# Two group sums in place of seven: the combine weights of the first 96 cells in a fused agent-attention and soft-MoE kernel

## The chip, the cores and the metric

The kernel runs on one core of one Trainium2 chip. The metric is the device time of one execution in microseconds; the figure for a kernel is the median of its runs. The core has a matrix engine (TensorE, PE in the profile), three engines for elementwise work (VectorE or DVE, ScalarE or ACT, GpSimd or POOL), and a sync engine (SP) from which all the transfers of this kernel are issued. Each engine works through its own queue of instructions in order, and waits on semaphores for the others.

## The reference

Two stages follow each other. First attention through 49 agents for each of 4 batches of 11,456 tokens of width 128, then a soft mixture of experts over all 45,824 tokens, with 8 experts of 4 slots each, so 32 slots:

```python
def sm(a, b):                      # softmax of scaled scores over the last axis
    s = scale * (a @ b.transpose(0, 2, 1))
    s = s - s.max(-1, keepdims=True)
    e = np.exp(s)
    return e / (e.sum(-1, keepdims=True) + 1e-09)
agent_v = sm(agents, k) @ v        # agents read the keys and values
x = (sm(q, agents) @ agent_v)      # queries read the agents
logits = x @ phi                   # 45824 x 32
d = softmax of logits over tokens  # dispatch weights
slot_input = d.T @ x
slot_out = relu(slot_input @ w1) @ w2        # expert by expert
c = np.exp(logits - logits.max(1, keepdims=True))
c /= c.sum(1, keepdims=True) + 1e-09         # combine weights of a token
out = c @ slot_out
```

The change concerns the last but one line: the sum of a token's 32 combine weights, and the division by it.

## The kernel before, in words

Tokens are handled in cells of 128; a batch has 90 cells, the four have 360. The tile `x_all` (128 partitions x 360 cells x 32 slots, fp32) holds the logits of all tokens, a token being one partition of one cell, and later, in place, their combine weights.

**The main stage.** Key groups of up to 20 cells (steps named k...) compute the agents' view of the values of a batch; query groups of up to 16 cells (steps q...) compute scores, softmax and logits. The steps that matter below: `ks` scores of keys, `km` and `kM` their maximum, `kr`/`kR` the running maximum, `ku`/`ke` subtract and exponential, `kE` the product with the values, `kA` its accumulation; `qs` scores of queries, `qt` their transposition, `qm` maximum, `qu`/`qe`/`qw` subtraction on POOL, exponential on ACT and sum on DVE (for every other group; the others do these in one ACT step, `qE`), `qr`/`qR` the reciprocal of the sum, `qg` the scaling on POOL, `qp`/`qc` transposition, `ql` the logits, `qM` their column maximum, `qn` their move into `x_all`. Per token, `cr` takes the maximum of the 32 logits, `cu` (POOL) subtracts it, `ce` (ACT) takes the exponential: from then on the cell holds combine weights that are not yet normalised. Per round of one or two query groups (13 rounds), `r1` to `r4` find the maximum over tokens, `ru` (POOL), `re` (ACT) and `rg` (PE) build the partial slot inputs, and `rc` stores them.

**The last steps before the output** are a chain: `nm`, `wt` (weights of the rounds), `l0`, `f0`/`f1`/`f2` (rescale of the earlier batches), `gl`, `gm` and `l1` to `l4` (the slot inputs, into `si`), `d0` to `d2` (the dispatch denominator), then per half of the experts and half of the hidden width `mh` (first product), `mr` (ReLU), `mt` (transposition), `mc` (copy), `mo` (second product), `ms`, `sb` and `sd`, which leaves the slot outputs in `sob`. `fl` are transpositions without use in TensorE's queue. `w1` and `w2` load the experts' weights once the last key group has released its buffers.

**The output stage** goes over 25 chunks of cells, `CHUNKS = [4, 12] + [16] * 21 + [4, 4]`, `C0` being the first cell of each. Of a chunk, `o_sum` (three DVE instructions: the sum over 32 slots, the addition of 1e-9, the reciprocal) and `o_mul` (POOL, multiplies in place) normalise the weights, `o_tr` (DVE) transposes them into one of four `ct` tiles, TensorE multiplies with `sob` into a PSUM tile `po`, DVE and ACT copy it to `ot`, and the sync queue writes it out. In the loop at the end (L994 to L1008) sums and multiplications run three chunks ahead and transpositions one.

The first chunks do part of this earlier, as steps of the written order: `os` (o_sum) and `om` (o_mul) for `NORM = 7` chunks (cells 0 to 95), `ot` (o_tr) for `EARLY = 4`. The sums lie in seven tiles `cd` of the pool that takes the place of the key buffers.

**What sets the order.** All steps up to the output loop are listed by hand in the string `ORDER`, in the form step.part@index. The order of issue on each engine is the order of its steps in this list; `_order` only asserts that every step comes behind those it depends on. Semaphores between the engines follow from the data. So to move a step in the string is to move it in its engine's queue. The costs written beside the steps are not used for the order.

Lines that the profile names: L252 scores of keys (`sk`), L351 `kE` (`ev`), L466 `qs` (`sq`), L472 `qt`, L477 `qm`, L494 `qE`, L504 `qr`, L535 `ql` (`lq`), L547 `qM` (`cm`), L552 `qn`, L560 `cr`, L563 `cu`, L568 `ce`, L635 `ru` (`dt`), L648 `rg` (`gp`), L652 `rc`, L726 `wt`, L734 `gl` (`g_all`), L757 `f0` (`fd`), L786 `l4` (`si`), L805 `mh` (`hp`), L811 the ReLU on DVE (`hs`), L818 `mt` (`htp`), L852 to L854 `o_sum` (`cd`), L859 `o_mul`, L865 `o_tr` (`ct`), L1002 `po`, L1006 and L1007 the copies to `ot`, L1008 the output.

Of the kernel before, what the change touches and what calls it, by code (L numbers as in the profile page):

```python
# [53 lines left out]
kM@3 kt kA qp.0@0 kr qx@3 qr@2 kt qR@2 qc.0@0 kR qg.0@2 kr qc.1@0 kb kR kn qg.1@2 ka@4 kb ku.0
qp.0@2 ka@3 kn ku.1 ke.0 kx@5 qp.1@2 qc.0@2 ku.0 kE.0@3 qc.1@2 ku.1 ke.1 qs.0@3 ke.1 ke.0
qs.1@3 kv@5 qt.0@3 kE.1 qt.1@3 qm@3 ks.0@5 kA qu@3 cx ks.1@5 km.0@5 qx@4 qe@3 kE.0@4 km.1@5
qw@3 kE.1 kM@5 qr@3 qR@3 kt kx@6 qg.0@3 kA kr kg.1 qg.1@3 kg.2 qp.0@3 kh.1 kh.2 kg.3 qs.0@4
kh.4 kh.3 kb kv@6 ql@0 qt.0@4 kn ql@1 ku.0 qc.0@3 qn.0@0 qs.1@4 ke.0 qM.0@1 qn.1@0 qM.0@0
kE.0@5 ku.1 qx@5 qM.1@0 ke.1 ks.0@6 qt.1@4 qm@4 kx@7 kE.1 km.0@6 qE.0 qM.1@1 ql@2 r1@0 kA r2@0
qn.0@1 ks.1@6 qM.1@2 qM.0@2 qn.1@2 kv@7 r3@0 qE.1 qp.1@3 qn.0@2 ru.0@0 km.1@6 qs.0@5 kM@6  # L60
qn.1@1 kt qt.0@5 ru.1 ks.0@7 kr kR cr@1 re.0@0 qr@4 qR@4 qx@6 re.1 cu@1 kb qs.1@5 km.0@7 kn
qc.1@3 rg.0@0 ku.0 qg.0@4 ka@6 rg.1 ce@1 ku.1 ql@3 ke.0 qg.1@4 qt.1@5 qp.0@4 ke.1 kx@8 qn.0@3
ks.1@7 qM.1@3 rc@0 qc.0@4 qm@5 qM.0@3 qu@5 r1@1 kE.0@6 km.1@7 qe@5 kM@7 cr@2 r2@1 kE.1 kv@8
r3@1 qn.1@3 ru.0@1 cr@3 qs.0@6 kA cr@0 cu@2 re.0@1 qs.1@6 qt.0@6 cu@0 qw@5 rg.0@1 ce@2 qx@7 kt
qt.1@6 ks.1@8 ru.1 ce@0 kr kR qr@5 qR@5 ka@7 qm@6 kb ks.0@8 cu@3 re.1 r4@1 kx@9 r4@0 kn qE.0
# [1003 lines left out]
```

## Time and profile before

| | |
|---|---|
| median of 3 runs | 320.97 us (319.19 to 323.69) |
| the profiled execution | 321.17 us |
| its span, first to last instruction | 318.9 us |
| busy: PE, DVE, ACT, POOL | 266.3, 248.1, 189.4, 132.5 us |
| HBM read, written | 79.91 MB, 23.59 MB |
| w1 issued first | 217.33 us from the span's start |
| first output issued | 258.21 us |

The span is the profile's own time axis; the profiled execution's time is 2.3 us longer than it. A timeline row gives start, length, engine, line, operation, tiles as out<-in with their shapes, and, in brackets, how long the engine sat idle before it and what ended that wait. A row with x2 or more merges instructions that followed each other. A row of a window gives the window, its length, then the busy time (and count) of PE, its weight loads, DVE, ACT and POOL, TensorE's granted clock, and the busy share and rate of the transfers. Releasers are inferred.

### The profile page before, as it was taken

The page shows a single profiled execution, that of the slowest core. Times are in us where ns is not written, and L with a number is a line of the kernel's source. Part 1 is how long each engine was busy: PE and PEld are TensorE (multiplying, and loading weights), DVE is VectorE, ACT ScalarE, POOL GpSimd, SP SyncE. Part 2 cuts the span into 40 slices and gives each one's busy share as a digit, 9 for nine tenths or more (in the row PEclk, how much of TensorE's full clock was granted, in tenths as well). Part 3 has the DMA queues.
Part 4 walks back from the last instruction along what each step waited for, and adds up shares of the span by engine and source line. Part 5 has one row for each costly group of instructions (what it writes and reads, how often), then busy time and mean ns, then how long its engine had stood idle before and what let it go on. Part 6 is the DMA issues. An engine that isn't in the chain of part 4 may idle for free.

```text
span 318.9 us, 11055 instructions
## 1 busy us (share of the span) xinstructions
PE 266.3 (84%) x4522; PEld 169.4 (53%) x4522; DVE 248.1 (78%) x598; ACT 189.4 (59%) x623; POOL 132.5 (42%) x166
## 2 busy tenths in 40 slices
PE   3799999997698998988999998998898876766850
...
GB/s 250 400 402 390 398 396 402 401 397 400 394 250 376 399 393 368 301 260 295 377 377 264 252 360 384 244 175 237 419 141 3 2 164 422 415 415 420 420 419 286
DMA packets 31298, 104.20 MB, mean 327 GB/s; under 512 B 3601, under 2 KB 7825, under 8 KB 27537
## 3 DMA queue, kind: packets, MB, share of 16 engines
...
HBM read 79.91 MB, written 23.59 MB: 325 GB/s over the span
## 4 chain that ended last, share of the span: by engine, by line
PE 45%; DVE 26%; DMA 10%; ACT 9%; issue 5%; POOL 2%; SPq 0%; DVEq 0%; POOLq 0%; ACTq 0%
PE sk L252 10%; PE ev L351 8%; PE sq L466 8%; DMA out<-ot 7%; PE tp L522 5%; ACT pt L494 4%; PE po L1002 3%; DVE pt L472 3%; PE lq L535 3%; DVE kmx L305 2%; ACT ot L1007 2%; DVE cd L852 2%; DVE ot L1006 2%; DMA w1s<-w 2%; DVE mx L477 2%
## 5 line engine op out<-in xcount | busy, mean ns | idle before, releaser
L494 ACT ACTIVATE pt<-pt,mx 128x49 f32<-128x49 f32 x192 | 61.6, 329 | 10.2 <-DVE mx L477 10.2
L513 POOL TENSOR_TENSOR pt<-pt,rt 128x392 f32<-128x392 f32 (+1 forms) x48 | 38.7, 809 | 46.1 <-DVE rt L508 25.2
L252 PE MATMUL sk<-ag,kt 128*64 128x49 f32 x1440 | 51.7, 230 | 6.6 <-DMA kt<-kT 4.3
L252 PEld LDWEIGHTS sk<-ag,kt 128*64 128x64 f32 x1440 | 48.8, 145 | 11.6 <-DVE ag L183 4.1
L466 PE MATMUL sq<-qt,ag 128*32 128x512 f32 (+1 forms) x384 | 49.6, 607 | 1.8 <-DVE et L339 1.1
L1002 PE MATMUL po<-ct,sob 32*128 32x512 f32 (+2 forms) x200 | 37.8, 838 | 15.6 <-DVE ct L865 11.3
L351 PE MATMUL ev<-vt,et 128*64 128x129 f32 x720 | 46.8, 277 | 1.7 <-issue 1.4
L1007 ACT COPY ot<-po 128x1536 f32<-128x1536 f32 (+2 forms) x25 | 32.8, 1311 | 23.3 <-DVE ot L1006 23.2
L351 PEld LDWEIGHTS ev<-vt,et 128*64 128x64 f32 x720 | 40.3, 138 | 9.6 <-issue 5.6
L472 DVE STREAM_TRANSPOSE pt<-sq 128x512 f32<-128x512 f32 (+1 forms) x48 | 31.9, 669 | 12.5 <-PE sq L466 12.0
L635 POOL TENSOR_TENSOR dt<-x_all,mbs 128x512 f32<-128x512 f32 (+1 forms) x24 | 29.2, 1227 | 28.8 <-DVE mbs L626 24.9
L859 POOL TENSOR_TENSOR x_all<-x_all,cd 128x512 f32<-128x512 f32 (+2 forms) x25 | 24.0, 961 | 38.0 <-DVE cd L854 37.3
L482 POOL TENSOR_TENSOR pt<-pt,mx 128x784 f32<-128x784 f32 (+1 forms) x12 | 16.2, 1353 | 55.4 <-DVE mx L477 53.1
L494 ACT ACTIVATION_READ_ACCUMULATOR pt<-pt,mx 128x1 f32 x192 | 37.0, 193 | 0.0
L529 ACT COPY pT<-tp 128x512 f32<-128x512 f32 (+1 forms) x48 | 25.7, 557 | 13.1 <-PE tp L522 11.0
L1002 PEld LDWEIGHTS po<-ct,sob 32*128 32x128 f32 x200 | 10.8, 247 | 42.5 <-ACT ot L1007 42.1
L522 PE MATMUL tp<-cs,pt 128*128 128x128 f32 x180 | 27.9, 286 | 5.9 <-issue 4.2
L305 DVE TENSOR_REDUCE kmx<-sk 128x49 f32<-128x490 f32 x32 | 20.7, 658 | 13.8 <-PE sk L252 13.6
L344 ACT ACTIVATE et<-et 128x490 f32<-128x490 f32 x36 | 21.6, 619 | 11.2 <-DVE et L339 11.1
L522 PEld LDWEIGHTS tp<-cs,pt 128*128 128x128 f32 x180 | 19.5, 142 | 15.1 <-issue 9.0
L339 DVE TENSOR_TENSOR et<-sk,kmb 128x490 f32<-128x490 f32 x36 | 22.5, 653 | 2.9 <-ACT kmb L329 2.8
L1006 DVE COPY ot<-po 128x512 f32<-128x512 f32 (+2 forms) x25 | 15.7, 629 | 11.4 <-DMA out<-ot 7.5
...
## 6 DMA issues: line engine op xcount, KB each, us to landing
...
```

What stands on the lines that cost most here:

```text
L252: t_.matmul(sp[r:r + 64, c - c0, :], xt[:, P * c + r:P * c + r + 64], ag[:, b, 0:A], start=True, stop=True)
L305: v_.tensor_reduce(out=o_, in_=sp.rearrange("p c a -> p a c"), axis=AX.X, op=ALU.max)
L351: t_.matmul(k["ev"][o_:o_ + 64, :], k["e"][:, c, :], k["v"][:, c, :], start=c < 2, stop=c >= n - 2)
L466: t_.matmul(q["s", h][32 * r_:32 * r_ + 32, :nt], ag[:, b, 32 * h:32 * h + 32], q["x"][:, r_, :], start=True, stop=True)
L472: v_.transpose(out=q["pt"][:, :n, 32 * h:32 * h + 32], in_=q["s", h][:, :nt].rearrange("p (t a) -> p t a", a=32))
L494: s_.activation(out=x, in_=x, func=AF.Exp, bias=q["mx"][:, c:c + 1], accum_out=q["dn"][:, c:c + 1])
L513: nc.gpsimd.tensor_tensor(out=x, in0=x, op=ALU.mult, in1=q["rt"][:, c0:c1].unsqueeze(2).to_broadcast([P, c1 - c0, A]))
L522: t_.transpose(q["tp", h][:, (c - c0) // 2, :], q["pt"][:, c:c + 2, :].rearrange("p c a -> p (c a)"), ident)
L529: s_.copy(out=q["pT"][:, c0 // 2:c1 // 2, :], in_=q["tp", h][:, :(c1 - c0) // 2, :])
L635: nc.gpsimd.tensor_tensor(out=q["dt"][:, :n], in0=q["lt"][:, :n, :], op=ALU.subtract, in1=mbs[:, ri, :].unsqueeze(1).to_broadcast([P, n, S]))
L1002: t_.matmul(po[:, r, :32 * n], z["sob"][32 * r:32 * r + 32, :], z["ct", j][32 * r:32 * r + 32, :32 * n], start=True, stop=True)
L1007: s_.copy(out=ov[:, 1:4], in_=po[:, 1:4, :32 * n])
```

## The change

The seven `os` steps become two, `os@0` for cells 0 to 47 and `os@1` for 48 to 95. Each is one reduction over 48 cells, one addition and one reciprocal, into halves of a new tile `cds` of 96 columns that exists from the kernel's start; so the sums no longer depend on `ms`, the step that sets up the tiles in the key buffers' place. They depend on the `ce` of the query groups that begin below cell 48 or 96. Both stand in the middle of the main stage: `os@0` between `qp.1@7` and `km.1@12`, `os@1` between `ks.0@13` and `kA`. The seven `om` steps follow one by one in the main stage: `om@0` and `om@1` around the `ru` of round 3 and `cu@6`, `om@2` behind `qg.1@11`, and `om@3` to `om@6` behind `qg.1@12` to `qg.1@15`. `om` of chunk 0 to 2 needs the first sum alone, the others need both.

Of the early transpositions, `ot@0` and `ot@1` now stand directly behind `l4` (the slot inputs) and ahead of `d1`, `ot@2` behind the first ReLU on DVE (`mr@32`), `ot@3` behind `mc@42`. Before, `os@3` and `om@3` stood some way ahead of `nm`, and the other six sums, the other six `om` and the four `ot` between `nm` and the second expert product. The order of all other steps is the same. The chunks from 7 on, in the output loop, are done as before, with a ring of seven `cd` tiles.

```diff
...
-fl r4@11 qn.1@21 rg.0@10 qn.0@21 fl cr@21 ru.1 re.0@11 fl fl fl nm os@1 wt fl rg.0@11 cu@21
-re.1 l0 fl f0 os@6 rc@11 f1 fl rg.1 om@1 ce@21 os@4 fl rc@10 fl gl om@6 ot@1 gm l1 d0 fl om@4
-fl l2 cr@18 fl l3 f2 l4 d1 cu@18 os@2 mh@35 d2 cu@20 ce@18 os@5 mh@31 mr@36 os@0 om@5 ce@20
-mh@39 mr@32 om@0 mt@41 ot@3 mt@37 mc@42 cu@22 mh@44 mc@38 ot@0 om@2 mr@40 mo ce@22 mr@45 ot@2
-mt@46 mt@50 mc@47 zz mo mc@51 mo ms mo sb ms sb fl fl sd
...
+qp.1@7 os@0 km.1@12 kn qg.1@10 qp.0@10 kM@12 qc.1@7 ku.0 kt kx@14 qs.0@11 ke.0 ku.1 kr ql@7 ke.1
...
+qs.1@11 r3@3 r4@3 ru.1 qp.1@9 om@0 qt.1@11 kb qm@11 qc.1@9 qp.1@8 ru.0@3 kn re.1 qs.0@12 ku.0 kv@13
+qc.1@8 ku.1 cu@6 om@1 re.0@3 ql@9 qt.0@12 ql@8 ke.0 qM.0@9 rg.0@3 cu@7 ce@6 qM.1@8 rg.1 qM.0@8 ke.1
...
+r4@4 kE.1 cr@9 qx@14 qr@11 qR@11 re.1 cu@9 qt.1@12 ks.0@13 os@1 kA qm@12 qg.0@11 ce@9 qp.1@10
+km.0@13 qE.0 qg.1@11 om@2 qp.0@11 qn.0@8 ks.1@13 cr@8 ru.0@4 qs.0@13 kx@16 km.1@13 cu@8 re.0@4 kM@13
...
+qn.0@21 fl cr@21 ru.1 re.0@11 fl fl fl nm wt fl rg.0@11 cu@21 re.1 l0 fl f0 rc@11 f1 fl rg.1 ce@21
+fl rc@10 fl gl gm l1 d0 fl fl l2 cr@18 fl l3 f2 l4 ot@0 ot@1 d1 cu@18 mh@35 d2 cu@20 ce@18 mh@31
+mr@36 ce@20 mh@39 mr@32 ot@2 mt@41 mt@37 mc@42 ot@3 cu@22 mh@44 mc@38 mr@40 mo ce@22 mr@45 mt@46
+mt@50 mc@47 zz mo mc@51 mo ms mo sb ms sb fl fl sd
...
+    cds = keep.tile([P, C0[NORM]], F32, name="cds")
...
+    def o_sums(h):
+
+        n = C0[NORM] // 2
+        x = cds[:, n * h:n * h + n]
+        v_.tensor_reduce(out=x, in_=x_all[:, n * h:n * h + n], axis=AX.X, op=ALU.add)
+        v_.tensor_scalar(out=x, in0=x, scalar1=EPS, scalar2=None, op0=ALU.add)
+        v_.reciprocal(out=x, in_=x)
+        for j in range(NORM):
+            z["cd", j] = cds[:, C0[j]:C0[j] + CHUNKS[j]]
+
     def o_sum(j):
...
-        z["cd", j] = wl(f"cd_{j}", [P, CHUNKS[j]], tag="cd", bufs=NORM)
+        z["cd", j] = wl(f"cd_{j}", [P, CHUNKS[j]], tag="cd", bufs=7)
...
+    def done(c):
+        return [k for k in ops if k[0] == "ce" and
+                groups[k[1]][0] * NCELL + GROUPS[groups[k[1]][1]][0] < c]
+
+    n = C0[NORM] // 2
+    ss = [op("os", (h,), "V", 2300, lambda h=h: o_sums(h), deps=done(n * h + n)) for h in range(2)]
     for j in range(NORM):
-        ends_ = [k for k in ops if k[0] == "ce" and groups[k[1]][0] * NCELL <= C0[j] + CHUNKS[j]]
-        f = op("os", (j,), "V", 800, lambda j=j: o_sum(j), deps=ends_ + [ms])
-        f = op("om", (j,), "G", 1000, lambda j=j: o_mul(j), deps=(f,))
+        f = op("om", (j,), "G", 1000, lambda j=j: o_mul(j), deps=ss[:1 + (C0[j] + CHUNKS[j] > n)])
         if j < EARLY:
-            op("ot", (j,), "V", 650, lambda j=j: o_tr(j), deps=(f,))
+            op("ot", (j,), "V", 650, lambda j=j: o_tr(j), deps=(f, ms))
```

The lines of the string show where the steps stand; the string was broken into lines anew, so a line of the new one holds other words than the old line in its place.

More of the change, by code (lines that the diff above doesn't have):

```diff
@@ L54 @@
[L54 to L65, printed above, removed]
@@ new lines @@
+kR ka@1 kb qs.0@1 kn ku.0 kv@0 ke.0 ku.1 qs.1@1 qt.0@1 ke.1 kE.0@1 kx@2 qt.1@1 qm@1 qs.0@0 qu@1
+kE.0@0 qt.0@0 kx@4 qs.1@0 qe@1 kA kE.1 qw@1 qt.1@0 ks.0@2 qr@1 qR@1 qm@0 qg.0@1 qx@2 ks.1@2 km.0@2
+qE.0 qg.1@1 kA qp.0@1 km.1@2 ks.0@4 kv@2 kM@2 qc.0@1 qp.1@1 km.0@4 qE.1 kt qs.0@2 kr kR kb kx@3
+qt.0@2 qc.1@1 qs.1@2 qr@0 qR@0 kn qg.0@0 ka@2 ku.0 ku.1 ks.1@4 ke.0 qg.1@0 qt.1@2 ke.1 kv@3 qm@2
+kE.0@2 km.1@4 qE.0 qp.1@0 kM@4 ks.0@3 kv@4 ks.1@3 km.0@3 qE.1 kE.1 km.1@3 kM@3 kt kA qp.0@0 kr qx@3
+qr@2 kt qR@2 qc.0@0 kR qg.0@2 kr qc.1@0 kb kR kn qg.1@2 ka@4 kb ku.0 qp.0@2 ka@3 kn ku.1 ke.0 kx@5
@@ new lines @@
+qp.1@2 qc.0@2 ku.0 kE.0@3 qc.1@2 ku.1 ke.1 qs.0@3 ke.1 ke.0 qs.1@3 kv@5 qt.0@3 kE.1 qt.1@3 qm@3
+ks.0@5 kA qu@3 cx ks.1@5 km.0@5 qx@4 qe@3 kE.0@4 km.1@5 qw@3 kE.1 kM@5 qr@3 qR@3 kt kx@6 qg.0@3 kA
+kr kg.1 qg.1@3 kg.2 qp.0@3 kh.1 kh.2 kg.3 qs.0@4 kh.4 kh.3 kb kv@6 ql@0 qt.0@4 kn ql@1 ku.0 qc.0@3
+qn.0@0 qs.1@4 ke.0 qM.0@1 qn.1@0 qM.0@0 kE.0@5 ku.1 qx@5 qM.1@0 ke.1 ks.0@6 qt.1@4 qm@4 kx@7 kE.1
+km.0@6 qE.0 qM.1@1 ql@2 r1@0 kA r2@0 qn.0@1 ks.1@6 qM.1@2 qM.0@2 qn.1@2 kv@7 r3@0 qE.1 qp.1@3 qn.0@2
+ru.0@0 km.1@6 qs.0@5 kM@6 qn.1@1 kt qt.0@5 ru.1 ks.0@7 kr kR cr@1 re.0@0 qr@4 qR@4 qx@6 re.1 cu@1 kb
@@ new lines @@
+qs.1@13 qE.1 qt.0@13 rg.0@4 qt.1@13 rg.1 kt qm@13 ks.0@14 kv@16 kr ce@8 qu@13 kR qr@12 qR@12 qc.0@11
+kb qs.0@14 km.0@14 kn rc@4 ka@13 qc.1@10 ku.0 qg.0@12 qp.1@11 qe@13 kt ku.1 ql@10 qg.1@12 om@3
+qc.1@11 qx@15 kr ke.1 qp.0@12 kR qn.0@10 ke.0 qM.0@10 ql@11 qM.1@10 qc.0@12 kb kE.0@13 qM.0@11 kn
+qM.1@11 ka@14 r1@5 qn.1@10 kx@15 cr@10 r2@5 kE.1 r3@5 qn.0@11 ru.0@5 ku.0 qs.1@14 kA ke.0 r4@5
+qn.1@11 cr@11 re.0@5 ru.1 qs.0@15 qt.0@14 qx@16 cu@11 rg.0@5 re.1 qw@13 qs.1@15 cu@10 ce@11 qr@13
+qR@13 rg.1 qt.1@14 kE.0@14 qg.0@13 rc@5 ce@10 qm@14 qx@20 qg.1@13 om@4 ks.1@15 kA qE.0 qt.0@15
@@ new lines @@
+qt.1@15 kg.2 kg.1 ks.0@15 qm@15 kv@15 kh.2 kh.1 qu@15 qE.1 qs.0@16 km.0@15 km.1@15 qs.1@16 kM@15
+qt.0@16 kt kx@19 qp.0@13 kr kh.4 qe@15 qr@14 qR@14 kb qt.1@16 qp.1@13 qg.0@14 kn qc.0@13 ku.0 kg.3
+kv@19 qp.1@12 qg.1@14 om@5 qc.1@13 qw@15 qp.0@14 ke.0 qp.1@14 kh.3 qr@15 qm@16 qc.1@12 qx@17 ks.0@16
+qc.0@14 qR@15 qc.1@14 ku.1 qg.0@15 ql@13 qE.0 km.0@16 ql@14 qg.1@15 om@6 qn.0@13 qp.0@15 qn.1@13
+qM.1@14 ks.1@16 qn.1@14 qM.0@13 qn.0@14 qE.1 qM.0@14 ql@12 kx@17 km.1@16 kE.0@15 qM.1@12 qM.0@12
+kM@16 qn.1@12 kt qn.0@12 qs.0@17 ke.1 kr cr@12 qp.1@15 qc.0@15 qr@16 qt.0@17 kE.1 qc.1@15 kR qR@16
@@ new lines @@
+kb qs.0@19 qt.1@18 qe@17 kn qm@18 qs.1@19 qx@21 qt.0@19 qE.0 rg.1 qw@17 ks.0@18 ku.0 ku.1 ks.1@18
+qx@23 km.0@18 rc@7 ke.0 qt.1@19 qs.0@20 qE.1 km.1@18 kM@18 qs.1@20 qm@19 kt qx@22 qt.0@20 qu@19
+kE.0@17 ke.1 kr kR qr@18 qR@18 ka@18 qt.1@20 qs.0@23 qg.0@18 qe@19 qm@20 kb kE.1 kn qg.1@18 ku.0
+qE.0 qs.1@23 qw@19 qp.1@18 qt.0@23 qp.0@18 kA ku.1 qs.0@22 qc.0@18 qr@19 qR@19 qt.1@23 qg.0@19 ke.0
+qs.1@22 qm@23 qE.1 qt.0@22 qu@23 ks.0@19 qt.1@22 qg.1@19 qm@22 qs.0@21 qc.1@18 qr@20 qR@20 kE.0@18
+km.0@19 qe@23 qg.0@20 ke.1 qw@23 kt qg.1@20 qE.0 qt.0@21 kE.1 kr kR qr@17 qR@17 qr@23 kb qp.0@20
@@ new lines @@
+qg.0@17 kA qR@23 qs.1@21 qg.1@17 kn qc.0@20 qg.0@23 ku.0 qp.0@17 ka@19 ke.0 qt.1@21 qg.1@23 qp.1@17
+qp.0@23 qc.0@17 qm@21 qc.1@17 kE.0@19 qE.1 qu@21 ql@17 w2 kA kg.2 qn.0@17 ms qM.0@17 kg.1 kh.2
+qp.0@19 kh.1 qr@22 kh.4 qR@22 qe@21 kg.3 qM.1@17 qp.1@19 qn.1@17 qg.0@22 w2 r1@8 kh.3 cr@17 qc.0@19
+r2@8 qw@21 ql@18 qc.1@19 qg.1@22 qp.0@22 r3@8 qc.0@23 qM.1@18 ru.0@8 qr@21 ql@19 qM.0@18 r4@8
+qn.1@18 w1 qc.0@22 qM.0@19 ru.1 qM.1@19 re.0@8 qp.1@20 r1@9 qR@21 cu@16 qn.0@19 re.1 r2@9 qc.1@20
+rg.0@8 qg.0@21 rg.1 ce@16 en@10 w1 ql@20 qn.0@18 en@11 qn.1@19 rc@8 qp.1@22 qM.0@20 cr@19 qp.0@21
```

88 lines of the change are left out of this document (28 added, 60 removed).

## Prediction

> **What bounds the kernel now.** I read four views, in this order: the page's slices, the windows, the timeline of each engine around the end of the main stage, and the waits. The end of the kernel comes first. The row of bytes moved in 40 slices of 8 us, and the row of output issues on the sync queue (start, length, count):
>
> ```profile
> GB/s 250 400 402 390 398 396 402 401 397 400 394 250 376 399 393 368 301 260 295 377 377 264 252 360 384 244 175 237 419 141 3 2 164 422 415 415 420 420 419 286
> ```
>
> ```profile
> 258.21 54.88 SPq L1008 DMA_DIRECT2D out<-ot  x25
> ```
>
> The output stage runs at 415 to 422 GB/s from its second full slice to the end: once the first output leaves at 258.21, transfers set the rest (128 rows of 46,080 fp32 values, 23.6 MB, take 56 us at 420). So the output stage moves as a block with its start. Before it stand two slices with 3 and 2 GB/s (239 to 255 us): the weights of the experts are in, nothing is written, and a chain of small steps leads to the first output. That gap is the place where this change can win. The windows show who is busy in it (PE, weight loads, DVE, ACT, POOL, clock, DMA share, GB/s):
>
> ```profile
> 240.00:250.00 10.00, 8.11 (x94) 4.62 (x98) 9.47 (x28) 2.64 (x6) 7.37 (x9) 1.00 0.01 2
> ```
>
> VectorE is busy 9.47 of 10 us. Its rows there, in time order (`cd` on L852 to L854 are the sums that the change moves; `fd` is f0, `g_all` gl, `si` l4, `hs` the first ReLU, mr):
>
> ```profile
> 239.05 0.83 DVE L757 TENSOR_SCALAR fd<-cs,wt 32x32 f32<-32x32 f32 x1
> ...
> 241.55 0.58 DVE L853 TENSOR_SCALAR cd<-cd 128x16 f32<-128x16 f32 x1
> 242.16 0.25 DVE L854 RECIPROCAL cd<-cd 128x16 f32<-128x16 f32 x1
> 242.33 0.25 DVE L734 TENSOR_TENSOR g_all<-g_all,wt 128x150 f32<-128x150 f32 x1
> ...
> 244.44 0.19 DVE L786 TENSOR_TENSOR si<-si_p,sie 128x32 f32<-128x32 f32 x1
> ...
> 247.20 0.97 DVE L853 TENSOR_SCALAR cd<-cd 128x4 f32<-128x4 f32 x1
> 248.21 0.18 DVE L854 RECIPROCAL cd<-cd 128x4 f32<-128x4 f32 x1
> 248.31 0.66 DVE L811 TENSOR_SCALAR hs<-hp 128x512 f32<-128x512 f32 x1
> ```
>
> Both steps of the real chain, gl and the ReLU, start right behind a sum. So the sums are on the path; how much is gained depends on what is late next.
>
> **What is removed.** Seven sums, 21 VectorE instructions. Prices by form, and the add alone (least/median/longest, ns):
>
> ```profile
> L477 DVE TENSOR_REDUCE mx<-pt 128x16 f32<-128x784 f32 x20 | 19.2, 959 | 0.7
> ...
> L852 DVE TENSOR_REDUCE cd<-x_all 128x16 f32<-128x512 f32 x21 | 14.1, 669 | 0.1
> ```
>
> ```profile
> L853 DVE TENSOR_SCALAR cd<-cd x25: 170/175/975, 225.5 to 303.0; 128x16 f32<-128x16 f32 x21, 128x4 f32<-128x4 f32 x3, 128x12 f32<-128x12 f32 x1
> ```
>
> A sum over 16 cells is 0.67 + 0.175 + 0.25 = 1.1 us. Five of these make 5.5. The two reduces give a slope of (959 - 669) / (784 - 512) = 1.07 ns an element, so the 12-cell sum is about 0.95 and the 4-cell one 0.6. Two of the adds were held: 0.58 and 0.97 against 0.175, 1.2 in all. Together 8.2 us leave VectorE from 225.5 on (the first add of that row): os@3 there, os@1, os@6, os@4 ahead of gl, os@2, os@5, os@0 between l4 and the ReLU. The seven multiplications om leave POOL there too:
>
> ```profile
> 236.04 2.68 POOL L635 TENSOR_TENSOR dt<-x_all,mbs 128x512 f32<-128x512 f32 x2
> 238.80 1.05 POOL L563 TENSOR_TENSOR x_all<-x_all,rms 128x512 f32<-128x512 f32 x1
> ...
> 247.10 1.05 POOL L859 TENSOR_TENSOR x_all<-x_all,cd 128x512 f32<-128x512 f32 x1 [0.72 <-DVE cd L854]
> 248.47 0.40 POOL L859 TENSOR_TENSOR x_all<-x_all,cd 128x128 f32<-128x128 f32 x1 [0.32 <-DVE cd L854]
> ```
>
> **How much of it the end sees: three pieces.**
>
> First, os@3. VectorE is 1.1 us earlier behind it, but soon needs a product of TensorE that does not move:
>
> ```profile
> 225.58 0.66 PE L535 MATMUL lq<-pT,bd_m 64*32 64x256 f32 x16
> ```
>
> ```profile
> 226.81 0.39 DVE L547 TENSOR_REDUCE cm<-lq 128x1 f32<-128x256 f32 x1
> ```
>
> The product ends at 226.24, and the maximum that reads it ran at 226.81. So only some 0.5 us pass on to what stands behind it on VectorE, the r3 of the last rounds among it, whose results start POOL's subtractions ru; these end, with cu, at 239.85. I take 0.5, with ends 0 and 1.1.
>
> Second, the sums ahead of gl. Without them gl waits for ScalarE's copy rc of round 10, which stands behind ce of cell group 21:
>
> ```profile
> 238.08 0.30 ACT L726 ACTIVATE wt<-m_all,nmx 128x5 f32<-128x5 f32 x1
> ...
> 239.88 0.63 ACT L568 ACTIVATE x_all<-x_all 128x512 f32<-128x512 f32 x1 [0.41 <-POOL x_all L563]
> 241.26 0.20 ACT L652 COPY g_all<-gp 128x50 f32<-128x50 f32 x1 [0.75 <-PE gp L648]
> ```
>
> The copy ends at 241.46, gl began at 242.33: 0.85 us for certain. The copy itself waited for TensorE (gp), which stood behind f1, which waited for f0, the `fd` row. f0 was late by os@1 and held until 239.88, while POOL's 238.80 row ran. Without os@1 it needs only the exponent wt (over at 238.38) and l0's short step, comes some 0.5 us sooner and can slip in at 238.72, between POOL's two rows; then ce, which ends at 240.51, is the last, and gl starts near 240.8: 1.5 us. I take 1.5, since f0 then arrives before the 238.80 row begins, with 0.85 as the low end.
>
> Third, the expert stage. TensorE's rows from the first `hp` on (three of the four products are in the 24 matmuls of the first row):
>
> ```profile
> 244.71 2.78 PE L805 MATMUL hp<-w1s,si 128*32 128x512 f32 x24
> 247.42 0.66 PE L818 MATMUL htp<-cs,hs 128*128 128x128 f32 x4
> 249.02 0.66 PE L818 MATMUL htp<-cs,hs 128*128 128x128 f32 x4 [0.95 <-DVE hs L811]
> 249.61 1.07 PE L805 MATMUL hp<-w1s,si 128*32 128x512 f32 x8
> ```
>
> The product that the 248.31 ReLU reads is the second of three, ready two thirds into the first row, at 246.6. VectorE is free by then: behind l4 (244.63) come ot@0 and ot@1, under 0.9 us together, and d2. So the ReLU starts 1.7 us earlier, the second `htp` follows the first at 248.1, and the fourth `hp` starts at 248.75 instead of 249.61: 0.86 us. Everything behind it to the first output is a chain through TensorE and shifts with it; ot@2 and ot@3 stand where VectorE waits for TensorE.
>
> Sum of the end: 0.5 + 1.5 + 0.85 = 2.85 us gained. Low end 0 + 0.85 + 0.85 = 1.7, high end 1.1 + 1.5 + 0.85 = 3.45.
>
> **What is added to the main stage.** Two group sums: a reduce of 48 x 32 = 1536 elements is 0.67 + 1024 x 1.07 ns = 1.76, the add about 0.2, the reciprocal by the slope from 0.18 (4 columns) to 0.25 (16) about 0.44: 2.4 us each. No row shows a reduce this long; the two ends are the slope and three times the 16-cell reduce (2.0), so 2.4 to 2.65. They stand where VectorE waited, once for `sk` and once for `ev`; these are the two longest waits of the rows for 120 to 220 us (total, times, longest):
>
> ```profile
> DVE kmx L305 <- PE sk L252: 3.3, 3, 1.8
> ...
> DVE acc L357 <- PE ev L351: 2.1, 2, 1.2
> ```
>
> os@0 overfills its hole by 0.6, os@1 by 1.2. The first two multiplications (4 and 12 cells, 0.40 and about 0.8 us, from the 0.40 row and a 16-cell price of 1.05) stand on POOL between the subtractions of round 3 and qu@11:
>
> ```profile
> 135.35 1.02 POOL L482 TENSOR_TENSOR pt<-pt,mx 128x490 f32<-128x490 f32 x1
> ```
>
> Behind qu@11 wait the exponential qe@11 and then VectorE's sum qw@11, and behind that in VectorE's order qr, qR, qt.1@12 and os@1 itself. So os@1 starts 1.2 late (more than the 0.6, not on top of it) and ends 2.4 us later than its successor kA used to start. kA's accumulator frees a PSUM buffer, and qm@12 behind it releases ScalarE's exponentials.
>
> The other five om stand in gaps of POOL, but they can hold small VectorE steps. In the trace this is the 0.97 add at 247.20: POOL's om of 247.10 ended at 248.15, and the add ended with it. Two such steps fall where an om will run:
>
> ```profile
> 151.98 0.16 DVE L321 TENSOR_TENSOR nm<-nr,nm 128x1 f32<-128x1 f32 x1
> ...
> 169.70 0.17 DVE L504 TENSOR_SCALAR dn<-dn 128x16 f32<-128x16 f32 x1
> ```
>
> At the price of the two held adds (0.4 and 0.8 over the median): 1.2.
>
> So VectorE is late by up to 2.4 + 1.2 = 3.6 us. The same two rows of waits hold 5.4 - 1.8 - 1.2 = 2.4 us more of idle time behind the two holes. If these take up the delay, 1.2 is left; if other waits do as well, nothing. Middle: 0.6, with ends 0 and 3.6.
>
> **A page and a row.** The Trainium skill, page "SBUF — State Buffer", section "Who interferes with whom", says that a tensor_scalar in a two-port mode, or an operation with two SBUF inputs, and a GpSimd instruction exclude each other for the whole instruction, and that tensor_reduce on trn2 never contends. The two held adds and the unheld reduces agree. By that rule the long reduces cost POOL nothing, and every om moved is a new chance to hold VectorE.
>
> **Rivals.**
> (1) The end does not see it: f0 stays held, POOL's chain does not move, and the main stage keeps 1.7 late. Gain 1.7 against 1.7: 321.0. For it: POOL is busy without a break to 239.85. Against: gl's 0.85 and the expert stage's 0.86 do not depend on POOL.
> (2) Slower: the seven om hold VectorE in the main stage. Place: each om beside a small two-input or scalar step of VectorE; price 0.6 each, 4.2 in all, with the 2.4 of os@1 and no later hole taking it up, less 2.85: +3.75, so 324.7. It decides when more than four of the seven meet such a step on the path; the rows above show two. The page's rule allows it, the timing speaks against it.
> (3) Much faster: VectorE alone sets the gap, nothing else is late next: 8.2 less the 0.9 of ot@0 and ot@1, less 0.6: 6.7 off, 314.3. Against it stand ACT's and PE's rows above.
>
> **The numbers.** Net 2.85 - 0.6 = 2.25 us off. The profiled execution took 321.17 us (span 318.9 and 2.3 around it): 318.9. The median of the three runs, 320.97, is 0.2 lower: 318.7. Chances: this forecast 0.68, (1) 0.18, (2) 0.07, (3) 0.05, the rest outside them. The range: 3.45 off with a free main stage gives 317.5; the three runs spread over 319.19 to 323.69, so I go 0.7 lower, 316.8; upward it holds (1) and part of the dearer main stage, 321.8. About 2% (6.4 us) is what a measurement of this kernel can tell from no change: faster needs (3), slower more than (2). Faster 0.05, same 0.93, slower 0.02.
>
> **What would show it.** Right: VectorE's longest wait for `sk` (1.8) is gone; in the gap of low GB/s gl starts 1.5 to 2.5 us earlier against the end of the main stage, no `cd` row stands between `si` and `hs`, the second `htp` follows the first without a wait, and the first output leaves 2 to 3 us earlier against the weights' first issue. The weights' first issue itself shows the main stage's price: 0 to 1.2 late. Wrong: that issue moves by more than 2.5, or the last step ahead of gl is still POOL's.

## The result, and the profile after

The change made the kernel slower by 0.6%: 322.62 us median (321.47 to 324.68) against 320.85 (318.63 to 323.99), 20 runs each, ratio 1.006 with a 95% interval of 1.0038 to 1.0082. That is 1.9 us, where 2.3 us of gain were forecast, and it lies outside the range. Measured again in a later group of runs (e12), the ratio was 1.0053 [1.001, 1.0097].

The profiled execution after took 324.39 us, span 322.6. It is one of the longest of the twenty, so the two profiles lie 3.2 us apart where the medians lie 1.8. Lines moved by a few: `sk` is L249, kA L354, `tp` L519, the sums (`cds`) L850 to L852, `om` L866, the output L1019. The sync queue's first issue of the weights and its output issues:

```profile
223.01 0.81 SPq L701 DMA_DIRECT2D w1s<-w  x2
...
261.24 54.70 SPq L1019 DMA_DIRECT2D out<-ot  x25
```

Before, these stood at 217.33 and 258.21. So the main stage ends 5.68 us later, and from there to the first output 38.23 us pass instead of 40.88: 2.65 won at the end, 5.68 lost ahead of it.

**The end** went as described. VectorE from f0 (`fd`) to the first ReLU (`hs`):

```profile
243.86 0.42 DVE L754 TENSOR_SCALAR fd<-cs,wt 32x32 f32<-32x32 f32 x1
246.42 0.32 DVE L731 TENSOR_TENSOR g_all<-g_all,wt 128x150 f32<-128x150 f32 x1 [2.14 <-ACT g_all L649]
...
248.59 0.19 DVE L783 TENSOR_TENSOR si<-si_p,sie 128x32 f32<-128x32 f32 x1 [0.27 <-PE si_p L780]
248.96 0.77 DVE L872 STREAM_TRANSPOSE ct<-x_all 128x128 f32<-128x128 f32 x2 [0.18 <-issue]
...
250.83 0.69 DVE L808 TENSOR_SCALAR hs<-hp 128x512 f32<-128x512 f32 x1 [0.85 <-PE hp L802]
```

No sum stands in between. gl comes 23.41 us after the weights' issue instead of 25.00; VectorE, busy for 9.47 of 10 us there before, now idles 2.14 in front of it, waiting for ScalarE's copy. TensorE's products, and the whole stretch as a window:

```profile
248.84 2.78 PE L802 MATMUL hp<-w1s,si 128*32 128x512 f32 x24
251.55 1.09 PE L815 MATMUL htp<-cs,hs 128*128 128x128 f32 x8
252.57 1.06 PE L802 MATMUL hp<-w1s,si 128*32 128x512 f32 x8
```

```profile
243.00:253.00 10.00, 9.82 (x138) 6.16 (x140) 5.71 (x19) 4.12 (x10) 5.36 (x5) 1.00 0.02 4
```

The two `htp` are one row of eight now, without a wait, and VectorE is busy 5.71 us: TensorE's row is the full one.

**The main stage** is where the time went. The two group sums on VectorE, with what stands ahead of the second, and kA:

```profile
122.76 1.75 DVE L850 TENSOR_REDUCE cds<-x_all 128x48 f32<-128x1536 f32 x1
124.54 0.19 DVE L851 TENSOR_SCALAR cds<-cds 128x48 f32<-128x48 f32 x1
124.77 0.45 DVE L852 RECIPROCAL cds<-cds 128x48 f32<-128x48 f32 x1
...
138.45 0.66 DVE L496 TENSOR_REDUCE dn<-pt 128x10 f32<-128x490 f32 x1 [1.21 <-ACT pt L484]
...
140.69 1.71 DVE L850 TENSOR_REDUCE cds<-x_all 128x48 f32<-128x1536 f32 x1
142.44 0.76 DVE L851 TENSOR_SCALAR cds<-cds 128x48 f32<-128x48 f32 x1
143.23 0.45 DVE L852 RECIPROCAL cds<-cds 128x48 f32<-128x48 f32 x1
143.60 0.25 DVE L354 SCALAR_TENSOR_TENSOR acc<-acc,al,ev 128x129 f32<-128x129 f32 x1
```

Before, the rows of qw@11 and kA on VectorE were these:

```profile
137.06 0.67 DVE L499 TENSOR_REDUCE dn<-pt 128x10 f32<-128x490 f32 x1
...
140.59 0.35 DVE L357 SCALAR_TENSOR_TENSOR acc<-acc,al,ev 128x129 f32<-128x129 f32 x1 [1.22 <-PE ev L351]
```

The first sum fits: what follows it is 0.3 late. Then qw@11 (138.45) is 1.39 late: 0.24 of it is left over from os@0 (the kA before stands at 130.36 instead of 130.12), the rest comes since the first two multiplications pushed qu@11 on POOL, the last row here, from 135.35 to 136.74:

```profile
132.21 0.40 POOL L866 TENSOR_TENSOR x_all<-x_all,cds 128x128 f32<-128x128 f32 x1
...
134.94 0.83 POOL L866 TENSOR_TENSOR x_all<-x_all,cds 128x384 f32<-128x384 f32 x1
...
136.74 1.02 POOL L479 TENSOR_TENSOR pt<-pt,mx 128x490 f32<-128x490 f32 x1
```

os@1 runs 2.9, its add held at 0.76 instead of 0.19 by the third multiplication:

```profile
142.10 1.05 POOL L866 TENSOR_TENSOR x_all<-x_all,cds 128x512 f32<-128x512 f32 x1
```

So kA starts at 143.60 instead of 140.59: 1.39 + 2.9 - 1.22 (the wait it fills) = 3.0 us late. kA reads the product `ev` out of one of only three PSUM buffers of the ring "a", and the query group's transposition `tp` on TensorE wants the next one. TensorE's rows after, and then the same work before:

```profile
143.99 0.63 PE L519 MATMUL tp<-cs,pt 128*128 128x128 f32 x4 [2.56 <-DVE acc L354]
144.55 2.28 PE L249 MATMUL sk<-ag,kt 128*64 128x49 f32 x40
146.76 2.57 PE L463 MATMUL sq<-qt,ag 128*32 128x512 f32 x16
```

```profile
141.63 1.09 PE L522 MATMUL tp<-cs,pt 128*128 128x128 f32 x8
142.66 1.37 PE L252 MATMUL sk<-ag,kt 128*64 128x49 f32 x40
143.96 1.93 PE L466 MATMUL sq<-qt,ag 128*32 128x512 f32 x16
```

TensorE waited 2.56 us, and then ran the same scores in 2.28 and 2.57 us instead of 1.37 and 1.93. The windows give the reason (columns as in the prediction, the clock is the third number from the end); after, then before:

```profile
140.00:145.00 5.00, 2.44 (x45) 2.01 (x43) 4.93 (x8) 0.87 (x2) 3.15 (x5) 0.97 0.20 72
145.00:150.00 5.00, 5.00 (x118) 3.08 (x114) 4.00 (x7) 5.00 (x31) 2.32 (x2) 0.69 0.39 113
```

```profile
140.00:145.00 5.00, 5.00 (x110) 4.10 (x108) 3.75 (x7) 3.41 (x19) 2.76 (x5) 1.00 0.23 88
145.00:150.00 5.00, 3.62 (x128) 2.73 (x120) 4.72 (x10) 3.72 (x21) 1.90 (x3) 1.00 0.98 352
```

After the wait the granted clock is 0.69. `sk` starts 1.89 late, less than the wait, because TensorE had come to it 0.85 earlier than before (140.78 against 141.63). The slower scores add 1.55, so the end of these `sq`, at 149.33, is 3.44 us late. From there the delay only grows. The two held steps of the prediction (0.16 and 0.17 before) start 3.5 and 3.9 late, and end 4.0 and 4.4 late:

```profile
155.44 0.68 DVE L318 TENSOR_TENSOR nm<-nr,nm 128x1 f32<-128x1 f32 x1
...
173.57 0.68 DVE L501 TENSOR_SCALAR dn<-dn 128x16 f32<-128x16 f32 x1
```

The last 1.3 us come up from 190 on, where TensorE stalls inside tiles with no wait that the profile shows (1.50 ahead of a `sk` at 202.06, where it was 0.93 before). These stalls differ from execution to execution; in the second profile of the change the weights' issue was 4.86 late instead of 5.68.

### The profile page after: what moved, and what is told of

Read it like the earlier page. It is cut to its first block, busy times and chain, and to the rows that moved or that the text cites. A ratio compares the mean times of both kernels' runs of the same rounds, so it can differ in the third digit from the quotient of the medians.

```text
span 322.6 us, 11040 instructions
## 1 busy us (share of the span) xinstructions
PE 266.2 (83%) x4522; PEld 170.8 (53%) x4522; DVE 246.9 (77%) x583; ACT 189.5 (59%) x623; POOL 132.2 (41%) x166
## 4 chain that ended last, share of the span: by engine, by line
PE 42%; DVE 26%; ACT 10%; DMA 9%; POOL 5%; issue 5%; SPq 1%; DVEq 0%; POOLq 0%; ACTq 0%
PE sk L249 9%; PE sq L463 8%; PE ev L348 7%; DMA out<-ot 7%; PE tp L519 4%; ACT pt L491 4%; DVE pt L469 3%; DVE ot L1017 3%; PE gp L645 2%; DVE mx L474 2%; PE lq L532 2%; DMA kt<-kT 2%; POOL dt L632 2%; DVE kmx L302 2%; ACT ot L1018 2%
## 5 line engine op out<-in xcount | busy, mean ns | idle before, releaser
L249 PE MATMUL sk<-ag,kt 128*64 128x49 f32 x1440 | 52.6, 232 | 8.4 <-DMA kt<-kT 4.9
L249 PEld LDWEIGHTS sk<-ag,kt 128*64 128x64 f32 x1440 | 49.6, 147 | 13.7 <-issue 5.1
L463 PE MATMUL sq<-qt,ag 128*32 128x512 f32 (+1 forms) x384 | 51.0, 601 | 2.3 <-DVE et L336 1.1
L1013 PE MATMUL po<-ct,sob 32*128 32x512 f32 (+2 forms) x200 | 35.8, 797 | 17.5 <-DVE ct L872 12.5
L491 ACT ACTIVATION_READ_ACCUMULATOR pt<-pt,mx 128x1 f32 x192 | 36.2, 189 | 0.0
L519 PE MATMUL tp<-cs,pt 128*128 128x128 f32 x180 | 27.8, 283 | 7.9 <-issue 4.0
L866 POOL TENSOR_TENSOR x_all<-x_all,cd 128x512 f32<-128x512 f32 (+1 forms) x18 | 17.6, 975 | 37.8 <-DVE cd L861 37.8
L519 PEld LDWEIGHTS tp<-cs,pt 128*128 128x128 f32 x180 | 19.2, 141 | 17.3 <-issue 9.7
```

The lines of the kernel that those rows point to most:

```text
L249: t_.matmul(sp[r:r + 64, c - c0, :], xt[:, P * c + r:P * c + r + 64], ag[:, b, 0:A], start=True, stop=True)
L463: t_.matmul(q["s", h][32 * r_:32 * r_ + 32, :nt], ag[:, b, 32 * h:32 * h + 32], q["x"][:, r_, :], start=True, stop=True)
L491: s_.activation(out=x, in_=x, func=AF.Exp, bias=q["mx"][:, c:c + 1], accum_out=q["dn"][:, c:c + 1])
L519: t_.transpose(q["tp", h][:, (c - c0) // 2, :], q["pt"][:, c:c + 2, :].rearrange("p c a -> p (c a)"), ident)
L1013: t_.matmul(po[:, r, :32 * n], z["sob"][32 * r:32 * r + 32, :], z["ct", j][32 * r:32 * r + 32, :32 * n], start=True, stop=True)
```

## The experiments

Theory at this point: os@1 ahead of kA keeps kA's PSUM buffer, TensorE waits for it, and nothing later takes the delay up; the multiplications lengthen that wait. Rival: the multiplications cost by themselves, by holding small VectorE steps wherever they stand. The diffs show pieces of the order string, or code lines, against the changed kernel. "Price" below is what the main stage costs by the ratio: (ratio - 1) x 320.9, plus 2.7 for the gain at the end. That gain hardly varies: from the weights' issue to the first output it is 37.93 to 38.32 us in every profile of a variant below, against 40.88 before. The change's own price is 4.6 by this. Each experiment's ratio, and so its price, is uncertain by about 1 us (e1's by 1.6).

**e1: neither sums nor multiplications of the first 96 cells.**

```diff
     def o_sums(h):
...
-        v_.tensor_reduce(out=x, in_=x_all[:, n * h:n * h + n], axis=AX.X, op=ALU.add)
-        v_.tensor_scalar(out=x, in0=x, scalar1=EPS, scalar2=None, op0=ALU.add)
-        v_.reciprocal(out=x, in_=x)
...
     def o_mul(j):
         n = CHUNKS[j]
+        if j < NORM:
+            return
```

> Leaves out the two group sums and the seven multiplications of the first 96 cells, so that only the emptied tail of the change is left. If the tail gains what the two traces show between the first weight issue and the first output (40.88 us before, 38.23 after: 2.65), and the main stage is as before, it comes to 320.85 - 2.65 = 318.2 us, the first weight issue stays near 217.3. If the tail's gain were itself only apparent (late work catching up), the time stays at 320 or more.

Measured 0.9895 [0.9845, 0.9945], 3.4 us off (1.8 to 5.0). The work that left the end is worth about this much once nothing is put in its place; all that the change loses is in the main stage. The weights' issue, expected near 217.3, came at 219.85 in the profiled execution, with 320.85 us the longest of the six: TensorE waited 2.73 us for a transfer of `qt` ahead of 202.97. Up to the kA at 188.70 it was on time (189.00 before).

**e2: the sums without the multiplications** (the second half of that diff alone).

> The group sums stay in the main stage, the seven multiplications are left out. Block theory (the second sum holds kA back, kA's PSUM buffer holds TensorE, and the lateness passes on to the end): 321.5 to 322.5 us, TensorE still waits over 2 us for DVE acc around 141 us. Multiplication theory (POOL's work in the main stage is the price): 318 to 319 us. An earlier qu@11 on POOL lets os@1 start up to 1.2 us sooner in either case.

**e3: the multiplications without the sums** (the first half alone, the tile `cds` set to ones).

> The seven multiplications stay in the main stage (by a tile of ones), the group sums are left out. Block theory: 318 to 319.3 us. Multiplication theory: 321.5 to 322.6 us.

Measured 0.9944 [0.9912, 0.9976] and 0.9942 [0.9909, 0.9975]: 1.8 and 1.9 us faster than before, prices 0.9 and 0.8. The block theory misses in e2, the multiplication theory in e3: either alone is cheap, together they cost 4.6. So it seems that neither "the sums" nor "the multiplications" is the cause by itself, and that the second of them pushes something over an edge. The surplus of both together over the two prices is 2.9 us (1.2 to 4.5, the intervals combined). Counted from e1's 3.4 in place of 2.7, as the expectation of e5 does (5.3 against 1.6 and 1.5), it is 2.2, and the interval then just reaches nothing (-0.1 to 4.5); the runs below have to bear it out. The sums alone, on VectorE (the add of the second one, then kA) and on TensorE:

```profile
141.69 0.19 DVE L851 TENSOR_SCALAR cds<-cds 128x48 f32<-128x48 f32 x1
...
142.29 0.25 DVE L354 SCALAR_TENSOR_TENSOR acc<-acc,al,ev 128x129 f32<-128x129 f32 x1
```

```profile
142.68 0.63 PE L519 MATMUL tp<-cs,pt 128*128 128x128 f32 x4 [1.12 <-DVE acc L354]
```

The same wait, but 1.12 instead of 2.56, and the clock stays at 1.00 from 140 to 150.

**e4: the second sum behind kA and qm@12.**

```diff
-qt.1@12 ks.0@13 os@1 kA qm@12 qg.0@11
+qt.1@12 ks.0@13 kA qm@12 os@1 qg.0@11
```

> All work as in the change, but the second group sum stands behind kA and qm@12 instead of ahead of kA. Block theory: TensorE's wait of 2.56 us for DVE acc goes, with the drop of its granted clock to 0.69 behind it: 1 to 2 us off the changed kernel, 320.6 to 321.6 us. If any 2.4 us on VectorE in the main stage cost 2.4 us wherever they stand, or if the multiplications are the price: 322.2 to 322.8 us.

Measured 0.9992 [0.9959, 1.0025], price 2.4: half of the loss is back. The wait for `acc` is gone, the clock stays at 1.00, and a wait of TensorE for ScalarE (1.53 ahead of a `gp` at 147.31) takes part of its place: 2.4 us of VectorE cost something behind kA too. kA is 0.16 later than before here, the next kA 1.69 (157.88 against 156.19).

**e5: the first two multiplications behind qu@11.**

```diff
-ru.1 qp.1@9 om@0 qt.1@11
+ru.1 qp.1@9 qt.1@11
...
-qc.1@8 ku.1 cu@6 om@1 re.0@3
+qc.1@8 ku.1 cu@6 re.0@3
...
-qs.1@12 qu@11 rc@3
+qs.1@12 qu@11 om@0 om@1 rc@3
```

> All work as in the change, but the first two multiplications stand behind qu@11 on POOL instead of ahead of it. Interplay theory (the price of sums and multiplications together, 5.3 us by the three runs so far against 1.6 and 1.5 alone, comes from the two multiplications that make the second sum 1.2 us later while it already holds kA back): qw@11 is on time, TensorE's wait for DVE acc falls from 2.56 to about 1.1 to 1.7, 1.2 to 2.2 us off the changed kernel, so 0 to 0.7 us under the kernel before. If the five later multiplications or the sum alone are the price: as the changed kernel, 1.5 to 2 us over the kernel before.

Measured 1.0045 [1.0014, 1.0077]: a miss. I took the push of qu@11 for what sets the two off; it is not enough to take it away. Its profile was a puzzle: it showed the fastest of its twelve executions (319.43 us; the median is 321.99), with a wait of 1.41 and the clock at 1.00. e14 below takes it up.

**e7: e4 and e5 together.**

> Both moves at once: the first two multiplications behind qu@11 and the second sum behind kA and qm@12. Interplay theory: no TensorE wait over 1.2 us near 142, the price left is at most that of the second sum's 2.4 us and the five later multiplications: 0.5 to 1.5 us under the kernel before. If the two moves cure the same loss and no other: as with one of them alone, 0 to 0.5 under the kernel before.

Measured 0.9976 [0.9942, 1.0009], price 1.9: little better than e4, and the intervals don't tell them apart. The profiled execution took 323.10 us, the longest of twelve (median 319.65). TensorE has no wait for `acc` in it and the clock stays at 1.00, and yet the weights leave at 222.08: kA is 2.8 late already, behind an idle stretch of TensorE of 1.83 ahead of an `ev` at 141.59 for which the profile shows no wait, and 1.6 more come up to the next kA, as in e4. So a single execution can be late without the wait for kA.

**e8: only the first sum, no second sum, no multiplications.**

> Leaves out the second group sum and the seven multiplications; the first group sum stays where the change has it. Both theories give the first sum only its 0.3 to 0.6 us of overhang over the hole it stands in: 2.5 to 3.3 us under the kernel before, as without any sum (3.4 under it). If every VectorE microsecond of the main stage costs one: 2.4 less gain, so 1.0 under the kernel before.

Measured 0.9907 [0.9872, 0.9942], 3.0 us off: within the uncertainty of e1. The first sum costs next to nothing where it stands; the sums' price is that of the second.

**e9: the third multiplication, which holds the add ahead of kA, moved to om@3.**

```diff
-km.0@13 qE.0 qg.1@11 om@2 qp.0@11
+km.0@13 qE.0 qg.1@11 qp.0@11
...
-ql@10 qg.1@12 om@3
+ql@10 qg.1@12 om@2 om@3
```

> The change with one multiplication (om@2, POOL) moved from behind qg.1@11 to directly ahead of om@3, so that it no longer runs beside the add of os@1; nothing left out. Theory H (POOL holds that add for 0.6 us ahead of kA, and kA holds TensorE): the add is 0.2 us, kA 0.6 us earlier, weights' first issue 0.5 to 1 earlier than in the change, ratio to before 1.002 to 1.004. Theory P (what counts is the push of qu@11 by the first two multiplications): no difference from the change, 1.006.

**e10: e5 and e9 together.**

> The change with the first two multiplications behind qu@11 and the third ahead of om@3: none stands ahead of kA on the way to it; nothing left out. If the muls act through kA's lateness alone, kA is late as with the sums alone (1.7 us), and the time is that of the sums alone plus the muls' other holds (0.5 to 1 us): ratio 0.996 to 0.999. If the muls cost whatever their place (their sum of work on POOL, the holds at nm and dn, the clock), it stays at 1.003 to 1.006.

Measured 1.001 [0.9968, 1.0053] for e9 and 0.9975 [0.994, 1.0009] for e10. By the ratios the holding of the add is worth 1.6 us of time (0.1 to 3.2), though the add itself is only 0.57 shorter; against the change as measured in the same group (e12) it is 1.4, within the uncertainty. In the profile the clock falls here too, the scores end 0.63 earlier than in the change (148.70 against 149.33), and the weights leave 2.55 earlier instead of the 0.5 to 1 expected, so most of this arises further on. With the push of qu@11 gone as well, 2.7 us are back (1.4 to 4.1). The add and kA in e9, and then TensorE's wait in e9 and in e10:

```profile
142.43 0.19 DVE L851 TENSOR_SCALAR cds<-cds 128x48 f32<-128x48 f32 x1
...
143.02 0.25 DVE L354 SCALAR_TENSOR_TENSOR acc<-acc,al,ev 128x129 f32<-128x129 f32 x1
```

```profile
143.42 0.69 PE L519 MATMUL tp<-cs,pt 128*128 128x128 f32 x4 [1.71 <-DVE acc L354]
```

```profile
141.54 0.63 PE L519 MATMUL tp<-cs,pt 128*128 128x128 f32 x4 [0.58 <-DVE acc L354]
```

2.56, 1.71, 0.58: the wait shrinks step by step as what makes kA late is taken away, with all the work still in the kernel.

**e12: the change once more.**

> The change as it is, for a second profiled execution. If the 2.56 us wait of TensorE ahead of kA's tile and the fall of the granted clock behind it belong to the change, both are there again (wait over 2 us, clock under 0.8 in 145 to 150 us). If they are this one execution's, the wait is 1 to 1.5 us and the clock 1.00, and the weights' first issue is under 221 us.

```profile
142.95 1.09 PE L519 MATMUL tp<-cs,pt 128*128 128x128 f32 x4 [2.84 <-DVE acc L354]
```

```profile
145.00:150.00 5.00, 5.00 (x83) 2.42 (x85) 2.13 (x5) 5.00 (x29) 2.09 (x2) 0.56 0.46 110
```

Both belong to the change: wait 2.84, clock 0.56.

**e13: the sums alone, the second reduce run twice.** No multiplication of the 96 cells is in it, so what it costs comes from the longer sum on VectorE.

```diff
-        v_.tensor_reduce(out=x, in_=x_all[:, n * h:n * h + n], axis=AX.X, op=ALU.add)
+        for _ in range(1 + h):
+            v_.tensor_reduce(out=x, in_=x_all[:, n * h:n * h + n], axis=AX.X, op=ALU.add)
```

> The sums alone (no multiplications of the 96 cells, so their weights stay unnormalised), with the reduce of the second group sum run twice: 1.75 us more of VectorE ahead of kA than with the sums alone (0.994). Theory kA: TensorE's wait ahead of the next tile grows from 1.12 to 2.5 to 3 us, its clock falls behind it, and the price is more than the 1.75: 320.5 to 322 (ratio 1.000 to 1.006). Rival, the delay passes on one to one with no fall of the clock: 320.3 (0.9995). Rival, it is the multiplications and not kA that make the change slow: most of the 1.75 is taken up later, 319 (0.996) or less.

Measured 1.003 [0.9993, 1.0067], 322.07 us; by the ratios 2.8 us above e2 (1.2 to 4.3, the two intervals combined), for 1.75 us of added work. The wait grew less than expected, and the clock fell as expected:

```profile
144.61 0.63 PE L519 MATMUL tp<-cs,pt 128*128 128x128 f32 x4 [1.91 <-DVE acc L354]
```

```profile
145.00:150.00 5.00, 5.00 (x79) 2.75 (x80) 4.31 (x7) 4.63 (x27) 2.32 (x2) 0.66 0.34 91
```

That most of the added work is taken up later (0.996) is excluded. Whether more than the 1.75 passes on, as the fall of the clock says, or just the 1.75 (0.9995), the interval doesn't decide. In the two profiles the scores end 3.51 us later than in e2 (149.97 against 146.46), 1.93 because they start later (145.17 against 143.24) and 1.58 because they run slower.

**e14: e5 once more, for a second profile.**

> The change with the first two multiplications behind qu@11, a second profiled execution of it (the first was its fastest: TensorE's wait 1.41 us, clock 1.00). If kA's wait decides, an execution of 321.5 or more shows a wait of 1.6 us or more and a granted clock under 0.9 in 142 to 150 us, and one under 320.5 again shows 1.4 or less and 1.00. If a slow execution shows the clock at 1.00 there, something else makes it slow.

Measured 0.9995 [0.9949, 1.0041] over eight executions of 317.74 to 321.78 us; the profiled one took 321.78. TensorE's wait and the window in this execution, and then the same two in e5's of 319.43:

```profile
144.10 0.63 PE L519 MATMUL tp<-cs,pt 128*128 128x128 f32 x4 [1.96 <-DVE acc L354]
```

```profile
145.00:150.00 5.00, 5.00 (x116) 2.63 (x112) 3.39 (x7) 5.00 (x30) 2.32 (x2) 0.66 0.52 157
```

```profile
143.30 0.63 PE L519 MATMUL tp<-cs,pt 128*128 128x128 f32 x4 [1.41 <-DVE acc L354]
```

```profile
145.00:150.00 5.00, 4.52 (x132) 2.76 (x128) 4.81 (x8) 5.00 (x30) 3.30 (x3) 1.00 0.64 182
```

The same kernel, 2.35 us apart, and the weights' issue 2.42 apart (221.46 and 219.04): the difference is all in the main stage. 0.8 of it stood there before (the kA before this one at 131.33 and 130.54); the other 1.6 comes behind the wait, where the scores take 1.70 + 3.21 us against 1.37 + 1.92. So the two profiles show both sides of the edge, as the theory says. That this is why the executions of this kernel differ is not shown: these are two of twenty, and the kernel before, which has no such wait in its profile, spread from 317.85 to 323.75 us beside e5. The two ratios of this kernel agree with each other from 1.0014 to 1.0041, so by how much it is slower than before, if at all, stays open.

All profiles together, in order of TensorE's wait for kA:

| kernel | wait for `acc`, us | clock, 145 to 150 us | weights' issue | ratio to before |
|---|---|---|---|---|
| before; e8; e6; e11 | none of note | 1.00 | 217.33; 217.68; 215.00; 215.56 | 1; 0.9907; 0.994; 0.9935 |
| e10 | 0.58 | 1.00 | 216.98 | 0.9975 |
| e2 | 1.12 | 1.00 | 219.60 | 0.9944 |
| e5 | 1.41 | 1.00 | 219.04 | 1.0045 |
| e9 | 1.71 | 0.77 | 220.46 | 1.001 |
| e13 | 1.91 | 0.66 | 221.10 | 1.003 |
| e14 (same kernel as e5) | 1.96 | 0.66 | 221.46 | 0.9995 |
| the change | 2.56 | 0.69 | 223.01 | 1.006 |
| e12 (the change) | 2.84 | 0.56 | 222.19 | 1.0053 |

e3 and e4 have no wait for `acc` in this list; their clock is 1.00 in the window, and the weights leave at 218.62 and 219.31. The same holds for e1 and e7, whose profiled executions were late elsewhere, as said above. Of the waits for `acc`, those up to 1.41 left the clock as it was, and from 1.71 it has fallen every time. The ratio, from all executions of a kernel, follows the order only roughly: the row shows one execution, in e5, e6 and e10 the fastest of its kernel.

**e6 and e11: the whole work at other places.** If kA is the place that must be kept clear, the sums should stand elsewhere. e6 has six chunks: cells 0 to 47 are summed behind kM@8, where VectorE waits at 86 us, with their four multiplications behind qt.1@7; cells 48 to 79 where the change has os@0, with om@4 and om@5 at its places of om@5 and om@6. e11 keeps seven chunks, with the first sum as in e6 and the chunks 4 to 6 summed one by one in VectorE's waits just ahead of the output.

```diff
-ke.0 kM@8 qx@8 qc.1@4 qs.1@7 qt.0@7
+ke.0 kM@8 os@0 qx@8 qc.1@4 qs.1@7 qt.0@7
...
-rc@1 ce@3 ql@4 ke.1 qt.1@7 kt
+rc@1 ce@3 ql@4 ke.1 qt.1@7 om@0 om@1 om@2 om@3 kt
```

> Complete work in other places: six chunks (80 cells) are done early instead of seven; cells 0 to 47 are summed behind kM@8, in VectorE's 4.05 us wait for qs before 89.9 us, and multiplied in the POOL gap behind qg.1@5 (84.7 to 95.1 us); cells 48 to 79 are summed where the change has its first sum (32 cells, 1.75 us against a hole of 1.8) and multiplied behind qg.1@14 and qg.1@15. No step then stands ahead of kA. If the main stage's price lies in place and not in the amount of work: 2 to 3 us under the kernel before, about 4 to 5 under the changed one. If VectorE and POOL time in the main stage cost their length anywhere: 0 to 1 over the kernel before.

> Nothing left out. First group sum (48 cells) in VectorE's wait behind kM@8 (85.9 us), its four muls on POOL behind qt.1@7; no second group sum: the chunks 4, 5 and 6 are summed one by one in VectorE's waits of the last 20 us of the main stage (behind mr@40, the first and the last sum of the squares of the output stage's tiles), each with its mul. Theory kA: no long sum stands ahead of kA, TensorE's wait ahead of kA's tile is under 0.5 us, main-stage price near 0, so the time is that of the change less 5: 317.3 (ratio 0.989), about 0.7 under the earlier early version (0.994). Rival: the three single sums fall into the end of the main stage, where VectorE is the bound, and cost their 3.3 us: 320 (0.997).

Measured 317.98 us, 0.994 [0.9909, 0.9972], and 318.07 us, 0.9935 [0.9897, 0.9973]. Both are faster than the kernel before by some 2 us and than the change by some 4, with all of the work done. TensorE's `tp` at this place, in e6 and in e11, has no wait:

```profile
139.72 1.10 PE L519 MATMUL tp<-cs,pt 128*128 128x128 f32 x8
```

```profile
139.89 1.10 PE L519 MATMUL tp<-cs,pt 128*128 128x128 f32 x8
```

e6 falls just short of its 2 to 3 us. e11 misses its 317.3 by 0.8; of the two ratios expected for it, 0.989 lies just outside the interval and the rival's 0.997 just inside, so the three single sums at the end may cost a part of their 3.3. So the change's idea holds; the places were wrong, that of the second sum above all (e8, e4). How much of the gain is due to the multiplications' new places, these two runs don't separate.

## Why the prediction was wrong

- **The end: right.** 2.85 predicted, 2.65 measured, inside 1.7 to 3.45. By pieces: 2.0 forecast up to gl, 1.6 measured (25.00 to 23.41); 0.85 in the expert stage, 1.1 measured (from gl to the fourth `hp` 7.28 before, 6.15 now). What was named as late next, ScalarE's copy behind ce, is what gl now waits for. Of the list of signs, all those on the end came true.
- **The prices of the added work: right.** 2.4 us a group sum, measured 2.4 when not held. os@0 overfills its hole by 0.5 (0.6 forecast): its place is reached 0.2 earlier than before and left 0.3 later. qu@11's push was 1.2 forecast, 1.39 measured at qw@11 with the 0.24 left over from os@0. The two held steps at `nm` and `dn` were there, 0.52 and 0.51 instead of 0.4 and 0.8. A third one was missed: om@2 starts right beside os@1 and holds its add by 0.57, so kA was 3.0 late and not 2.4.
- **The step that failed** is the one behind it: "If these take up the delay, 1.2 is left; if other waits do as well, nothing. Middle: 0.6, with ends 0 and 3.6." They did not take it up. The price was 4.6 by the ratio and 5.68 in the profile, above even the upper end, and the weights' issue moved by more than the 2.5 that the prediction had named as the sign of being wrong. I added up VectorE's idle time over the next 70 us and let the delay run into it. But that idle time belongs to waits for TensorE, and TensorE was late itself by then: kA's PSUM buffer stood in its way. e2 shows what such waits do take up: VectorE is 1.70 late at kA there, TensorE 0.58 at the `sk` behind its wait (143.24 against 142.66), and the next kA is 0.58 late. VectorE's delay shrank to TensorE's, and no further. The sentence "kA's accumulator frees a PSUM buffer" is in the prediction; who wants this buffer next was not followed up. Had it been, a wait of TensorE of about 1 us would have been in the sum, worked out from the trace of before: with a delay of 2.4, kA ends at 143.3, and TensorE's first four `tp` end at 142.3.
- **What was not in the sum at all** is the clock. After the wait it was 0.69 and, in e12, 0.56, and the next scores took 1.6 us longer in the profile (2.28 + 2.57 against 1.37 + 1.93), nearly half of the 3.44 lost at this place. The kernel's own trace showed this ahead of time, on TensorE and in the windows of before:

```profile
86.42 1.54 PE L522 MATMUL tp<-cs,pt 128*128 128x128 f32 x8 [2.32 <-issue]
```

```profile
87.50:90.00 2.50, 2.50 (x15) 0.66 (x17) 0.07 (x1) 2.50 (x10) 0.00 (x0) 0.50 0.81 308
```

A wait of 2.32 us, and 0.50 behind it. I did not look for such a row. It would have given a chance and not a sure price: in the change the wait at this place is 2.30, and the clock behind it 1.00.
- **The hole itself** was less than I took it for. VectorE's wait of 1.22 ahead of kA in the trace of before ends with `ev`, and `ev` was late by one of TensorE's stalls inside a tile (1.44 at 138.79). In the change that stall was 0.34 and in e10 0.89; with the shorter stall TensorE also comes earlier to the buffer that kA holds. A hole that is seen in one execution may not be there in the next.
- **The rivals.** (2), at 0.07, had the right sign and the wrong mechanism: three of the multiplications held VectorE at 0.5 each, not more than four at 0.6; e3 shows the seven by themselves at a price of 0.8. The delay "with no later hole taking it up" was its true half. (1) and (3) did not happen.
